# Attention and a routed expert layer on one core: the opening pair in halves, the overflow region moved into a product, the last product cut in columns

## The chip, the cores and the metric

The kernel runs on one core of a Trainium2 chip. A core has a matrix engine (TensorE, PE in the profile; its weight loads are listed apart as PEld), a vector engine (VectorE, DVE), an activation engine (ScalarE, ACT), a general engine (GpSimd, POOL) and a queue engine that mainly starts transfers (SyncE, SP). Each engine works through its own list of instructions in order, and the lists meet only through semaphores. PSUM is the memory that TensorE writes; it is used here in banks of 512 floats per partition.

The metric is the device time of one execution in microseconds. Before the change it is 694.73 us, the median of three runs (694.60 to 694.82).

## The reference

The output is computed in two blocks. Attention comes first, over 4 batches, 8 heads, 768 positions and 64 features. Every query and every key is given to the one of 16 centroids of its head that it resembles most, and a query attends only to keys of its own cluster:

```
q_assign = argmax(q_n @ c_n)          # 16 clusters for each head
k_assign = argmax(k_n @ c_n)
scores   = where(q_assign == k_assign, scale * q @ k.T, -1e9)
attn     = softmax(scores);  x = attn @ v
```

The result, laid out as 3072 rows of 512, goes to a router with 8 experts:

```
expert_idx = argmax((xn @ en.T) / tau);  gate = softmax(...)[expert_idx]
out[row]   = gate * (relu(x[row] @ w1[expert_idx]) @ w2[expert_idx])
```

All inputs are float32. How many rows an expert gets depends on the data.

## The kernel before, in words

**Attention.** The heads are taken two at a time: 4 batches times 4 head pairs are 16 pairs, n = 0 to 15. A pair has 12 units: two halves of the queries (hq, 384 each) by six groups of 128 keys (j). For one unit `scores` (L497) writes a two-bank PSUM tile with two kinds of product. Part 1 is q times k. Part 0 is a bf16 product of code tables (`t["H"]`) that adds a large negative number wherever the clusters differ. `expo` (L526) takes the exponential on ACT into one of six `probs` buffers, and `attend` (L531) multiplies with v on PE and adds the row sums on DVE.

**Preparation of a pair.** Before its scores a pair needs turned q and k, the products with the centroids, the choice of a centroid for every row and the code tables. These are the pieces of `prep_pieces` (L365). For pairs 1 to 15 the pieces are spread over the loop of the pair before (`between`, L1378), q and k are turned by DVE in blocks of 32, and the table is turned by a transposing DMA. Pair 0 has nothing to hide behind: `begin` (L327) does its pieces one after the other, turns q and k with PE (`turn`, L374), multiplies with the centroids (`products`, L403), chooses (`choose`, L422, four DVE instructions on 384 columns), writes codes (`codes`, L435), and turns the table with PE (`turn_numbers`, L459). Then the table's copies, the part 0 products and the first exponentials follow. `keep_up` (L229) issues matmuls whose results nobody reads.

**The order of the work** is written out by hand: under `tc.manual_schedule` every engine's list is the order in which the Python code issues instructions. The main loop after `begin()` takes two units in each step: scores of the two units after next, exponentials, the pieces of `between`, then `attend` of two units. Units 0, 1 and 2 have their scores in `begin`; unit 3 comes in the first step. PSUM is shared out by pools: `psS` has two tiles of two banks (tag `s_ps`), `psO` one, and `misc()` hands out two single banks in turn.

**Experts.** Rows are gathered from the DRAM tensor `x_rows` and results are scattered to `out` by indirect DMAs, which POOL issues. The list `later` has 16 items: "sized" items take one expert each with up to 272 rows, and "block" items take 128 rows of any one expert. Item 13 is a block (positions counted from 0), item 14 the smallest sized item (160 rows) and item 15, the last, is a block. For a block, `hidden` (L1299) computes the 1024 hidden values into two PSUM banks, with one ACT Relu each, and `result` (L1318) multiplies with w2 into one bank `y_ps`, scales on ACT into a tile `y` (three buffers) and scatters. A sized item runs `sized_hidden` (L1210): eight groups (f = 0 to 7) of four products, each group into its own bank, evicted by an ACT Relu (L1227). Three banks come from `psH`, every fourth group goes to `psX`. The weights of an item are in slot 0 or 1 of `w1s` and `w2s`, loaded by SP (2 MB each).

**The overflow region.** If more rows must be placed in blocks than the eight block items can hold, `overflow` (L1589) processes up to 14 more ("whole") items under `tc.If(n_used > KX)`. With these inputs the branch isn't taken. Every engine still loads the count, compares, branches, and then passes a short list of semaphore instructions that stand for the work of the region (these have line L1605, and the loads of the count L1590): first it waits until its own earlier work is done, then it raises its counters to the values that they would have after the region. POOL's list waits for every earlier scatter and gather to land, and ends with an instruction named INC_SWDGE_SEM that raises the counters of the indirect DMAs. Whatever comes after the region and touches a buffer which the region may use waits for the raised counters. In the kernel before, the region is called at L1630, at the head of item 14; the weight loads of item 15 follow it.

Of the kernel before, what the change touches and what calls it, by code (L numbers as in the profile page):

```python
# [18 lines left out]
P = 128  # L19
# [20 lines left out]
def kernel(  # L40
# [143 lines left out]
    def load(n, names):  # L184
        b, hp = pairs[n]
        t = ld.setdefault(n, {})
        for nm in names:
            x = t[nm] = ldp.tile([P, NJ, 2, D], F32, tag=nm + "32", name=nm + "32")
            for h in range(2):
                rows = {"q": q, "k": k, "v": v}[nm][b, 2 * hp + h]  # L190
                if nm == "v":

                    r = rows.rearrange("(i j a t) d -> a i t j d", i=2, a=2, t=SQ)
                    for g in range(P // SQ):
                        nc.sync.dma_start(
                            out=x[SQ * g : SQ * g + SQ, :, h], in_=r[g // 2, g % 2]
                        )
                    continue
                if n == 0:

                    for i in range(1 + (nm == "k")):
                        js = slice(NJ // 2 * i, NJ // 2 * i + NJ // 2) if nm == "k" else slice(0, NJ)
                        queue = nc.scalar if nm == "k" and i == 0 else nc.sync
                        queue.dma_start(
                            out=x[:, js, h], in_=rows.rearrange("(j p) d -> p j d", p=P)[:, js]
                        )
                    continue


# [42 lines left out]
    def constants():  # L252
        nc.vector.memset(onesb, 1.0)
        keep_up(10, idle_ps[:, 0])
# [45 lines left out]
    def unit_centroids():  # L300
        unit_rows(cn_r)
        nc.vector.tensor_scalar(cn2, bc(c_sb, [P, 2, D], 1), cn_r, None, ALU.mult)
        bk = misc()
# [8 lines left out]
    def unit_experts():  # L312
        unit_rows(en_r)
        nc.vector.reciprocal(tau, tau)
        nc.vector.tensor_scalar(emb, emb, en_r, tau, ALU.mult, ALU.mult)

    def turned_experts():
        bk = misc()
        for c in range(KD):
# [3 lines left out]
        nc.vector.tensor_copy(  # L323
            embT[:, :, 0:E], bk[:, 0 : KD * E].rearrange("p (c e) -> p c e", e=E)
        )

    def begin():  # L327

        nc.scalar.dma_start(out=c_sb, in_=centroids.rearrange("h c d -> (h c) d"))
        load(0, "q")  # L330
        load(0, "k")
        nc.sync.dma_start(out=emb, in_=moe_expert_emb)
        nc.sync.dma_start(out=tau, in_=moe_tau.to_broadcast([E, 1]))
# [4 lines left out]
        nc.scalar.activation(en_r, epsc[0:E], ACTF.Sqrt)  # L338
        norm_rows(cn_r, c_sb, P)
        unit_centroids()  # L340
        piece(0, "turn0")
        piece(0, "turn1")
        norm_rows(en_r, emb, E)

        nc.scalar.activation(cn_r, epsc, ACTF.Exp)
        piece(0, "products")
        for m in range(2):
            scores(m, (1,))
        un[2]["s_ps"] = psO.tile([P, 2, 512], F32, tag="o_ps", name="s_ps2")
        scores(2, (1,))  # L350
        piece(0, "choose")
        piece(0, "codes")
        keep_up(6, misc())
        unit_experts()
        rest = piece(0, "turn_numbers")
        next(rest)
        for m in range(3):
            scores(m, (0,))
        next(rest, None)
        turned_experts()  # L360
        for m in (0, 2, 1):
            expo(m)
        token_numbers()

    def prep_pieces(n):  # L365
# [8 lines left out]
        def turn(nm, half):  # L374
# [12 lines left out]
            if nm == "q":  # L387
                (nc.vector.tensor_copy if half else nc.scalar.copy)(
                    t["qT"][:, HS * half : HS * half + HS], bk[:, 0:HS]
                )  # L390
            else:
                (nc.scalar.copy if half else nc.vector.tensor_copy)(
                    in_halves(t["kT"])[:, half], bk[:, 0:HS].rearrange("p (s t) -> p s t", t=SQ)
                )
# [27 lines left out]
        def choose():  # L422
# [3 lines left out]
            amax = smp.tile(shp[0:2], F32, tag="amax", name="amax")  # L426
            sel = smp.tile(shp, BF16, tag="sel", name="sel", bufs=1)
            pm = smp.tile(shp[0:2], BF16, tag="pm", name="pm")
# [6 lines left out]
        def codes():  # L435
            pm = t["pm"]
            nc.scalar.activation(cd[..., 1], pm, ACTF.Copy, scale=wcd)
            for i, p0 in enumerate((0, D)):
                g = slice(p0, p0 + D)
                if n == 0:  # L440
                    nc.vector.scalar_tensor_tensor(
                        out=cd[g, :, :, 2 * i],
# [6 lines left out]
                    continue  # L449
# [4 lines left out]
            if n > 0:  # L454
                nc.sync.dma_start_transpose(
                    out=t["H"], in_=cd.rearrange("p s h c -> p (s h c)")
                )

        def turn_numbers():  # L459

            U = S // (4 * SQ)
            bks = []
            for half in range(2):
                bk = misc().bitcast(BF16)
                for u in range(U):
                    nc.tensor.transpose(
                        bk[:, P * u : P * u + P],
                        cd[:, U * half + u].rearrange("p h c -> p (h c)"),
                        identb,
                    )  # L470
                bks.append(bk[:, 0 : P * U].rearrange("r (s x) -> r s x", x=P))
            H = [t["H"][:, U * half : U * half + U] for half in range(2)]
            nc.vector.tensor_copy(H[0][:, :, 0:SQ], bks[0][:, :, 0:SQ])
            nc.scalar.copy(H[0][:, :, D:], bks[0][:, :, D:])
            nc.vector.tensor_copy(H[1][:, :, 0:SQ], bks[1][:, :, 0:SQ])
            yield
# [822 lines left out]
    def hidden(it, halves=(0, 1)):  # L1299

        d = mo[it]
        for half in halves:
            if half == 0:
                d["hT"] = mop.tile([P, F], F32, tag="hT", name="hT")
# [415 lines left out]
```

## Time and profile before

| quantity | value |
|---|---|
| median of three runs | 694.73 us (694.60 to 694.82) |
| the profiled execution's own time | 695.09 us |
| its span, first to last instruction | 693.3 us |
| granted TensorE clock | 0.999 |
| TensorE busy | 684.1 us, 99% of the span |
| VectorE, ScalarE, GpSimd busy | 381.8, 262.6 and 266.2 us |
| DMA traffic | 135.55 MB, 196 GB/s on average |

The profile is of one execution. Its own time is 1.8 us longer than its span; that is what lies outside the first and last instruction. A line such as "L518 PE MATMUL" is a group of instructions by the line of the kernel that issued them, the engine and the operation. In a timeline a row gives start and length in us, the engine, the line, the operation and its tiles, how many instructions are merged in it and, in brackets, how long the engine was idle before and who ended that. The chain of waits follows the last instruction back from releaser to releaser.

### The profile page before, as it was taken

The numbers are of one execution on the slowest core, as the hardware profiler recorded it, in microseconds if no ns is written. First come the engines' busy times: TensorE is split into PE (matmuls) and PEld (weight loads), VectorE is DVE, ScalarE is ACT, GpSimd is POOL, SyncE is SP. The second block draws the span as 40 slices with busy tenths as digits, with TensorE's granted clock in tenths as the row PEclk, the third lists the DMA queues.
The fourth block names the chain that finished last, engine by engine and source line by source line (L and its number), as shares of the span: only waits on it lengthen the run. The fifth ranks groups of instructions, "written<-read, shape, count | busy, mean of one in ns | idle before, by whom it ended". The sixth has DMA issues, their size and how long they took to land.

```text
span 693.3 us, 16291 instructions
## 1 busy us (share of the span) xinstructions
PE 684.1 (99%) x6517; PEld 459.3 (66%) x6517; DVE 381.8 (55%) x667; ACT 262.6 (38%) x443; POOL 266.2 (38%) x494
## 2 busy tenths in 40 slices
PE   8999999999999999999999999999999999999996
PEld 4444444444444444455866778888979797979694
DVE  5789898999989999988564122140211303030310
ACT  5666665577656765576224120101010111111111
POOL 2122221321232212343315343576656465646502
PEclk9999999999999999999999999999999999999999
DMA  8755556875577588699699957457777686879450
GB/s 133 123 93 105 101 94 95 155 144 103 106 138 157 99 163 162 182 261 271 176 318 359 353 211 269 136 182 283 281 273 279 205 301 228 301 256 315 155 225 32
DMA packets 244157, 135.55 MB, mean 196 GB/s; under 512 B 207840, under 2 KB 207842, under 8 KB 244076
## 3 DMA queue, kind: packets, MB, share of 16 engines
q1 hardware_dynamic: 237116, 121.10, 64.3%
q0 software_dynamic: 6016, 13.12, 5.4%
q8 instruction: 54, 0.88, 0.6%
q10 hardware_dynamic: 944, 0.23, 0.2%
q14 instruction: 27, 0.22, 0.1%
HBM read 115.92 MB, written 13.12 MB: 186 GB/s over the span
## 4 chain that ended last, share of the span: by engine, by line
PE 91%; issue 3%; DMA 3%; POOL 1%; DVE 1%; POOLq 0%; ACT 0%; DVEq 0%
PE s_ps L518 22%; PE o_ps L540 18%; PE h_ps L1309 10%; PE y_ps L1325 10%; PE h_ps L1220 9%; PE y_ps L1258 6%; PE misc L1258 5%; PE x_ps L1220 3%; DMA out_dram<-ys,spidx 3%; PE misc L590 2%; PE misc L411 2%; PE misc L669 1%; PE idle_ps L232 1%; POOL xin L1078 0%; POOL out_dram L1089 0%
## 5 line engine op out<-in xcount | busy, mean ns | idle before, releaser
L529 ACT ACTIVATE prob<-s_ps 128x768 f32<-128x768 f32 x192 | 154.1, 814 | 100.7 <-PE s_ps L518 99.7
L518 PE MATMUL s_ps<-qT,kT 64*64 64x384 f32 x1536 | 155.6, 482 | 0.0
L540 PE MATMUL o_ps<-prob,v 64*64 64x385 f32 x1536 | 141.1, 483 | 0.0
L559 DVE TENSOR_TENSOR acc<-acc,prob 128x768 f32<-128x768 f32 x128 | 121.7, 951 | 8.5
L540 PEld LDWEIGHTS o_ps<-prob,v 64*64 64x64 f32 x1536 | 58.1, 133 | 65.2 <-issue 57.6
L1309 PE MATMUL h_ps<-xTm,w1s 128*128 128x128 f32 x768 | 88.5, 275 | 0.0
L1309 PEld LDWEIGHTS h_ps<-xTm,w1s 128*128 128x128 f32 x768 | 87.5, 192 | 1.4 <-issue 1.0
L1267 DVE STREAM_TRANSPOSE ys<-y_ps 128x256 f32<-128x256 f32 (+4 forms) x16 | 6.2, 404 | 147.0 <-PE y_ps L1258 119.1
L1325 PE MATMUL y_ps<-w2s,hT 128*128 128x512 f32 x192 | 84.5, 593 | 0.0
L518 PEld LDWEIGHTS s_ps<-qT,kT 64*64 64x64 f32 x1536 | 55.2, 133 | 36.9 <-issue 32.3
L574 POOL COPY behind<-acc 1x1 f32<-1x1 f32 x30 | 6.7, 223 | 178.2 <-DVE acc L559 169.3
L1220 PE MATMUL h_ps<-xTs,w1s 128*128 128x272 f32 (+7 forms) x384 | 72.9, 346 | 1.1 <-ACTq L1605 1.1
L1220 PEld LDWEIGHTS h_ps<-xTs,w1s 128*128 128x128 f32 x384 | 66.6, 190 | 8.0 <-issue 2.4
L1316 ACT ACTIVATE hT<-h_ps 128x512 f32<-128x512 f32 x24 | 14.3, 596 | 149.1 <-PE h_ps L1309 121.5
L1089 POOL DMA_INDIRECT out_dram<-ys,spidx x56 | 56.2, 1004 | 35.5 <-DVE ys L1282 18.3
L518 PE MATMUL s_ps<-hot 64*64 64x384 bf16 x768 | 64.2, 325 | 1.0 <-DVE hot L477 0.7
L1078 POOL DMA_INDIRECT xs<-x_rows,gpidx x56 | 56.9, 1016 | 18.7 <-issue 18.1
L1325 PEld LDWEIGHTS y_ps<-w2s,hT 128*128 128x128 f32 x192 | 35.6, 190 | 40.2 <-issue 39.9
L518 PEld LDWEIGHTS <-hot 64*64 64x64 bf16 x768 | 23.8, 106 | 43.9 <-issue 41.8
L1258 PE MATMUL misc<-hTs,w2o 128*128 128x272 f32 (+7 forms) x256 | 48.2, 346 | 0.0
L1258 PE MATMUL y_ps<-hTs,w2o 128*128 128x272 f32 (+7 forms) x256 | 48.0, 346 | 0.0
L1258 PEld LDWEIGHTS misc<-hTs,w2o 128*128 128x128 f32 x256 | 44.4, 190 | 2.7 <-issue 0.2
(274 smaller groups left out, 711.0 us busy)
## 6 DMA issues: line engine op xcount, KB each, us to landing
w1s<-in_moe_w_dram SPq DMA_DIRECT2D x18, 2048.0 KB
w2s<-in_moe_w_dram SPq DMA_DIRECT2D x18, 2048.0 KB
v<-in_v_dram SPq DMA_DIRECT2D x128, 48.0 KB
k<-in_k_dram SPq DMA_DIRECT2D x62, 96.0 KB
q<-in_q_dram SPq DMA_DIRECT2D x60, 96.0 KB
x_rows<-xb SPq DMA_DIRECT2D x60, 96.0 KB
xr<-x_rows SPq DMA_DIRECT2D x9, 512.0 KB
w1s<-in_moe_w_dram SPq DMA_DIRECT2D x4, 1024.0 KB
```

The costliest lines, as they stand in the source:

```text
L411: nc.tensor.matmul(bk[2 * C * i : 2 * C * i + 2 * C, 0:HS], lhsT=cnB[:, hp], rhs=r, start=True, stop=True,)
L518: nc.tensor.matmul(s_ps[D * half : D * half + D, h, 0:HS], lhsT=l[rows, half], rhs=r[rows], start=part == (1 if len(parts) < 2 else 0), st ...
L529: nc.scalar.activation(d["prob"][:, :, 0:HS], d["s_ps"][:, :, 0:HS], ACTF.Exp, scale=scale)
L540: nc.tensor.matmul(g["o_ps"][D * h : D * h + D, half, 0:HE], lhsT=ld[n]["v"][keys, j, h], rhs=d["prob"][keys, h, 0:HE], start=(j == 0), st ...
L559: nc.vector.tensor_tensor(g["acc"], g["acc"], d["prob"][:, :, 0:HS], ALU.add)
L1078: nc.gpsimd.indirect_dma_start(out=to, out_offset=None, in_=of, in_offset=bass.IndirectOffsetOnAxis(ap=at, axis=0), bounds_check=n - 1, oo ...
L1089: inst = nc.gpsimd.indirect_dma_start(out=to, out_offset=bass.IndirectOffsetOnAxis(ap=at, axis=0), in_=of, in_offset=None, bounds_check=n - 1,
L1220: nc.tensor.matmul(bk, lhsT=w1s[it.slot][:, c, P * f : P * f + P], rhs=d["xT"][:, c, 0:C], start=(c == 0), stop=(c == KD - 1),)
L1258: nc.tensor.matmul(bks[g][:, 0:C], lhsT=d["w2"][:, f, P * g : P * g + P], rhs=d["hT"][:, f, 0:C], start=(f == 0), stop=(f == KF - 1),)
L1309: nc.tensor.matmul(bk[:, m : m + P], lhsT=w1s[it.slot][:, c, f0 + m : f0 + m + P], rhs=d["xT"][:, P * c : P * c + P], start=(c == 0), stop ...
L1316: nc.scalar.activation(d["hT"][:, f0 : f0 + 512], bk, ACTF.Relu)
L1325: nc.tensor.matmul(bk, lhsT=d["hT"][:, P * c : P * c + P], rhs=w2s[it.slot][:, c], start=(c == 0), stop=(c == KF - 1),)
```

## The change

Three things change, with some moves that go with them.

1. **The first pair in two halves.** `load` takes pair 0's q and k in halves of 384 rows, all on SP's queue: q first half, k first half, q second half, k second half. v of pair 0 is loaded in the order of its rows, with one DMA for each head instead of four. emb and tau are loaded from ACT's queue. `turn` becomes one piece for each matrix and half and returns its copy, so that `begin` says which engine makes it. kT keeps the rows' order. `half_products`, `choose(half)` and `codes(half)` work on half of the columns; the middle code is computed by POOL instead of ACT for pair 0. The second half's products go to a bank of their own (`c_ps`, in a tile of `psS`). `table(half)` turns six code blocks in two banks of three, with one copy of each bank, where `turn_numbers` had five copies. For pair 0 the part 0 product takes the half's table, so a unit of the first query half needs the first half's table of queries. `begin` interleaves the halves, and only units 0, 2 and 1 are scored there; unit 3's scores now stand between the two `attend` calls of the first step. `keep_up` issues 8 matmuls at the start instead of 10, and the second call, of 6, is gone. The scaling of the experts' embedding goes to one ACT instruction, its copy from PSUM too. `products` of pair 1 move from the first step's end into the second step, and `token_numbers` moves from `begin` to the fifth step.
2. **The region inside a block's second product.** `overflow` is called in item 13 between the two halves of `result`. Inside the region "whole" items use the buffers of others for their hidden values and results (`hTs`, `h_ps`), item 13's slot of weights, and reload half of item 13's w2 at the end. The tile `y` of item 13 is taken in the second half of `result`, and so after the region.
3. **The last product in 384 and 128 columns.** Item 15 uses `result_last`: eight products into one bank for columns 0 to 383, an ACT instruction for these, eight products into the other bank for the last 128 columns, an ACT instruction for those, then the scatter.

The core of the diff:

```diff
+                    for half in halves:
+                        js = slice(NJ // 2 * half, NJ // 2 * half + NJ // 2)
+                        nc.sync.dma_start(out=x_h[:, js], in_=rows[:, js])
...
-        keep_up(10, idle_ps[:, 0])
+        keep_up(8, idle_ps[:, 0])
...
-        piece(0, "turn0")
-        piece(0, "turn1")
-        norm_rows(en_r, emb, E)
-        nc.scalar.activation(cn_r, epsc, ACTF.Exp)
-        piece(0, "products")
-        for m in range(2):
-            scores(m, (1,))
...
-        keep_up(6, misc())
-        unit_experts()
-        rest = piece(0, "turn_numbers")
-        next(rest)
-        for m in range(3):
-            scores(m, (0,))
-        next(rest, None)
-        turned_experts()
-        for m in (0, 2, 1):
-            expo(m)
-        token_numbers()
+        piece(0, "turn", "q", 0)(nc.vector.tensor_copy)
+        piece(0, "turn", "k", 0)(nc.scalar.copy)
+        turned_centroids()
+        unit_experts()
+        nc.scalar.activation(emb, emb, ACTF.Copy, scale=en_r)
+        piece(0, "half_products", 0)
+        piece(0, "turn", "q", 1)(nc.scalar.copy)
+        ld[0]["c_ps"] = psS.tile([P, 2, 512], F32, tag="s_ps", name="c_ps")
+        piece(0, "turn", "k", 1)(nc.scalar.copy)
+        turned_experts()
+        junk = smp.tile([P, 1], F32, name="junk1", bufs=1)
+        nc.scalar.activation(junk, epsc, ACTF.Exp)
+        piece(0, "choose", 0)
+        piece(0, "codes", 0)
+        scores(0, (1,))
+        piece(0, "half_products", 1)
         un[2]["s_ps"] = psO.tile([P, 2, 512], F32, tag="o_ps", name="s_ps2")
         scores(2, (1,))
+        evicts = piece(0, "table", 0)
+        evicts[0](nc.vector.tensor_copy)
+        evicts[1](nc.scalar.copy)
+        scores(0, (0,))
+        expo(0)
+        piece(0, "choose", 1)
+        piece(0, "codes", 1)
+        scores(2, (0,))
+        expo(2)
+        scores(1, (1,))
+        evicts = piece(0, "table", 1)
+        evicts[0](nc.vector.tensor_copy)
+        evicts[1](nc.scalar.copy)
+        scores(1, (0,))
+        expo(1)
...
             for m in range(i, i + 2):
                 attend(m)
+                if m == 0:
+                    scores(3, (1,))
+                    scores(3, (0,))
+                    expo(3)
...
+    def result_last(it):
+        d = mo.pop(it)
+        y = mop.tile([P, DM], F32, tag="y", name="y", bufs=3)
+        cols = [slice(0, DM - P), slice(DM - P, DM)]
+        for cut in cols:
+            bk = bank("y_ps", psY)
+            for c in range(KF):
+                nc.tensor.matmul(bk[:, cut], lhsT=d["hT"][:, P * c : P * c + P],
+                    rhs=w2s[it.slot][:, c, cut], start=(c == 0), stop=(c == KF - 1))
+            nc.scalar.activation(
+                y[:, cut], bk[:, cut], ACTF.Copy, scale=it.gates[:, it.col : it.col + 1])
+        scatter(out[:], it.tables[2][:, it.col : it.col + 1], y, N)
...
+                own.e = expert_of(own)
+                load_part(w2s[own.slot], moe_w2, own.e, KF, 1, 2)
...
             if i == LAST - 1:
-                overflow()
                 weights1(later[LAST])
                 weights2(later[LAST])
...
-                result(it)
+                result(it, (0,))
+                if i == LAST - 2:
+                    overflow()
+                result(it, (1,))
...
-                result(it)
+                result_last(it)
```

## The prediction, made before the change was run

> **What bounds the kernel now.** I read the page first, then the chain of waits over the opening and the timelines of both ends.
>
> The page's first part:
>
> ```profile
> PE 684.1 (99%) x6517; PEld 459.3 (66%) x6517; DVE 381.8 (55%) x667; ACT 262.6 (38%) x443; POOL 266.2 (38%) x494
> ```
>
> TensorE is idle for only 9 us of 693, but part of its busy time in the opening computes nothing. The chain of waits from 0 to 32 us (start, length, what):
>
> ```profile
> 1.07 4.45 PE idle_ps L232 x10
> ...
> 7.85 1.22 PE misc L411 x8
> 9.07 0.02 issue
> 9.09 0.59 DVE asn L420
> ...
> 13.80 0.38 DVE hot L477
> 14.18 0.03 issue
> 14.20 0.39 PE s_ps L518 x4
> 14.59 0.02 issue
> 14.61 0.82 ACT prob L529
> 15.43 0.04 issue
> 15.47 1.00 PE s_ps L518 x12
> ...
> 18.91 1.74 PE s_ps L518 x24
> 20.65 1.29 PE o_ps L540 x16
> ```
>
> From 9.09 to 14.20 the chain runs on DVE: transpose, choice, codes, table copies. From 18.91 on, PE is without a gap, so the start of the second step's `attend` (20.65) is my clock for the opening: what comes earlier there comes off the end. The timeline of the tail:
>
> ```profile
> 654.92 0.69 ACT L1336 ACTIVATE y<-y_ps,slot_gates 128x512 f32<-128x512 f32 x1 [4.12 <-PE y_ps L1325]
> 655.17 0.39 SPq L1128 DMA_DIRECT2D w1s<-in_moe_w_dram  x1
> 655.89 0.97 POOL L1089 DMA_INDIRECT out_dram<-y,sidx  x1 [1.94 <-ACT y L1336]
> 655.99 3.53 PE L1220 MATMUL h_ps<-xTs,w1s 128*128 128x160 f32 x24 [1.10 <-ACTq L1605]
> ...
> 687.69 0.69 ACT L1336 ACTIVATE y<-y_ps,slot_gates 128x512 f32<-128x512 f32 x1 [4.65 <-PE y_ps L1325]
> 688.65 0.97 POOL L1089 DMA_INDIRECT out_dram<-y,sidx  x1 [7.43 <-ACT y L1336]
> ```
>
> At the region PE waits for ACT, which must first do item 13's scaling. The instructions of L1605:
>
> ```profile
> L1605 POOLq EVENT_SEMAPHORE  x5: 17/43/43, 656.7 to 665.4; - x5
> L1605 PEldq EVENT_SEMAPHORE  x1: 51/51/51, 655.1 to 655.1; - x1
> L1605 POOLq INC_SWDGE_SEM  x1: 1230/1230/1230, 665.4 to 665.4; - x1
> ```
>
> POOL stays in the region until 666.7 and nobody minds, since nothing behind it is wanted before 675.
>
> **What the skill says.** "TensorE: Matmul & The Clock Gate", Part 1, gives 426.7 ns between 512-column matmuls while the clock is cold and 215.7 ns warm. The trace agrees: L232's first ten are 427 ns apart, the six at 11.1 us 216 ns; the switch falls at about 5.95 us. "DMA: Bandwidth & Descriptors", section "Issuing engines are not separate DMA queues", says that transfers of all engines run on the same 16 DMA engines and interleave. The trace agrees, harshly: an indirect DMA issued alone has raised its semaphore 2.1 to 2.5 us later, one issued just after a 2 MB weight load after 5.4 to 6.5 us (581.41 to 587.04 behind the load of 579.93; 562.73 to 568.52 behind 561.53). "Runtime: NRT & Kernel Launch", "Instruction fetch mechanics", says a taken branch can stall on a fetch; here ACT's branch at 655.46 is followed by its next instruction at 655.92.
>
> **The opening.** I re-time the new order with measured durations; a half costs about half plus the fixed part (0.55 to 0.30).
> - Eight `keep_up` end at 1.07 + 8 x 0.427 = 4.5. SP's half loads (0.5 us of issue each; 786 KB of q and k had landed by 7.0) land q's first half at about 3.7, k's at 4.9, the second halves at 6.0 and 7.2. Emb and tau precede nothing urgent on ACT; two k loads of 0.5 us leave that queue.
> - Six cold transposes (0.213) and the centroids' end at 6.16. DVE copies q (0.56) and the centroids (0.46) until 6.64. Half products then take 0.55, so DVE's transpose runs 7.2 to 7.55, choice and codes (0.30+0.31+0.21+0.30 and 2 x 0.2, with gaps) to 9.25. Before, the same point was 12.48.
> - ACT meanwhile: expert scaling to 7.6 (0.62), copies of q and k to 8.6 (0.48 each), embT 0.2, exp table load 1.28, ready at 10.3. PE scores units 0 and 2 between, table transposes end about 10.2, DVE's copy 10.4, ACT's 10.8. Unit 0's part 0 follows, its exponential ends at 12.0 (before: 15.43).
> - ACT then runs unit 2 (0.81), a table copy (0.48) and unit 1 to 14.15. PE has `attend` 0, unit 3's scores, `attend` 1 by 14.9, then scores 4 and 5 to 16.5 and pair 1's products (0.85). Those need pair 1's k turned by DVE (0.97), landed at 16.8 before. SP starts that load 2.9 us sooner, since v takes 2 issues instead of 8 (5.25 us); at the rate of before (786 KB in 6.2 us behind v) it lands about 15.5, turned by 16.5. The second `attend` starts about 17.35.
>
> That is 3.3 us before 20.65. A schedule on paper misses handoffs, so I take 0.6 off: **-2.7**. Bounds: -3.3, and -1.2 where pair 1's k lands when it did. Moving `token_numbers` (four DVE instructions, 0.7 us in all) costs nothing as DVE idled 2.8 us before 29.45; without that cover it delays an accumulation that has six buffers of lead. Removing the six `keep_up` frees 1.5 us of PE time that was waiting anyway. A cold clock for one more window would cost about 1 us.
>
> **The region.** (a) PE's last y matmul started at 654.30; the next could have started at 654.73 and started at 655.99: 1.26 us lost. New: the first half's end is 3.44 us earlier and ACT is through (its Relu ended 650.81), so only drain, branch and restart remain: counter raised 0.8 us after the last start (655.10 against 654.30), first load about 0.3 later: 0.76 lost. **-0.5**, between -0.1 and -0.7. The SP list has passed by 647.2.
>
> (b) The new wait. `y` of item 13 is taken after the region, and whole items use all three y buffers. So ACT's scaling waits for raised scatter counters, hence for POOL's region; the program of before shows this wait at item 15's scaling, where POOL is long through. Behind it on ACT stand the eight Relus of item 14, and PE needs the first of them for its fifth group, having four banks. When does POOL pass? Its last scatter before the region goes out at 652.98 and landed at 655.15. But SP's load of w1 for item 15 is held only by PE's passing: it went 0.08 us after PE's counter, so it goes at about 651.73 now, ahead of that scatter instead of behind it. With the delay behind a load, 6.1 us, it lands at 659.1. POOL then took 1.51 us from landing to raised counter (665.16 to 666.68): 660.6. ACT scales (0.69), first Relu (0.30), hops: PE goes on at 661.7. It would get to its fifth group 4.45 us (as from 655.99 to 660.44) after 655.5: 659.95. Stall 1.8 us, **+1.8**; bounds 0 (landing in 2.2 us) and 5 (the 9.3 us that item 13's own scatter took). SP's second load waits for the product's end as before; the scatter of y moves behind the region on POOL, where 10 us of slack cover it.
>
> **The last product.** Its 16 matmul records are 0.429 us apart. Cut: 16 x 0.322 (the spacing of 384 columns in L518) + 16 x 0.112 (128 columns, L1309) = 6.95 against 6.87: +0.08. The second hidden half is wanted 2.6 us after the start, 683.2, and was there at 683.05. The scaling on the path falls from 0.69 to about 0.28 (0.30 for 160 columns, L1227), the first hides behind 1.8 us of products: -0.41. Together **-0.3**, between -0.45 and +0.1.
>
> **The sum.** -2.7 - 0.5 + 1.8 - 0.3 = -1.7. The profiled execution has a span of 693.3 and its own time 695.09; these become 691.6 and 693.4. Its 695.09 is 0.36 above the median 694.73, so the median becomes 693.0.
>
> **The rivals.** The kernel's measurement tells 0.2% (1.39 us) from nothing; 693.34 and 696.12 are the bounds.
> - *No wait at y* (0.22): the scatter slips past the load or ACT gets by. Against it: every scatter of the trace issued after a load waited over 5 us. -3.5: 691.2.
> - *The opening stays bound by transfers* (0.15): pair 1's k or DVE's queue holds the second step, -1.2 instead of -2.7. For it: DMA engines were 0.95 busy from 12 to 24 us; against it, SP's earlier start. 694.5.
> - *Slower* (0.13): the scatter lands as late as the one of 655.89 did, 9.3 us after issue, at 662.3. Then POOL passes at 663.8, PE stalls 5.0: 696.2. It decides from 660.8 on, 7.8 us after issue, where the opening's gain is eaten.
>
> **How the numbers follow.** My forecast (0.50) spans 692.0 to 694.3, two thirds under 693.34. Faster: 0.34 + 0.22 = 0.56. Same: 0.16 + 0.15 + 0.02 = 0.33. Slower 0.11. The range 690.9 to 695.6 leaves out a little of the first rival and most of the last.
>
> **What would show it.** First exponential's end near 12.0 and the second step's `attend` near 18; at item 13 a branch gap of 0.8 us; ACT's y a few us after its product, right after INC_SWDGE_SEM, with a gap on PE between the fourth and fifth group of item 14; a last scaling of 0.28 us. Wrong if y starts with its product, or if DVE's turn of pair 1 ends after 17.

## The result and the profile after

| quantity | before | after |
|---|---|---|
| median, 22 runs of each | 694.60 us | 691.63 us |
| lowest and highest | 694.39, 695.16 | 691.41, 695.12 |
| ratio after to before, 95% interval | | 0.9964 (0.9956 to 0.9972) |
| profiled execution: own time, span | 695.09, 693.3 | 691.77, 690.0 |
| second step's `attend` starts | 20.65 | 18.51 |
| item 13's first product with w2 starts | 647.85 | 645.65 |
| item 14's first product starts | 655.99 | 653.06 |
| last scatter is handed over | 688.65 | 685.38 |

The kernel became 2.97 us faster; the forecast was 1.7 us. Of the 22 executions after, 19 lie between 691.41 and 691.99 and three at 695.00 to 695.12. And the gain doesn't come out the same in every measurement: a later one, told below, gave 693.73 us on a chip where the kernel before takes 694.59. Both have to be explained.

Line numbers from here on are those of the kernel after. `attend` is L576, the scores are L554, the y products L1389 and L1366, the scalings L1400 and L1373, item 14's first product L1256, the region L1677. First the page's line for TensorE and the others:

```profile
PE 681.5 (99%) x6533; PEld 461.2 (67%) x6533; DVE 381.3 (55%) x668; ACT 264.2 (38%) x447; POOL 267.3 (39%) x496
```

There are 16 more matmuls than before, 2.6 us less busy time and a span 3.3 us shorter, so idle time on TensorE shrank by only 0.7 us. Most of the busy time that went did nothing: the two products on zeros that the start lost took 0.85 us, and the six of the second `keep_up` 1.47 us. The chain of waits of the opening (start, length, what) answers to the one shown of before:

```profile
1.06 3.60 PE idle_ps L232 x8
...
9.62 0.81 PE s_ps L554 x8
10.43 0.29 PE misc L502 x3
...
10.81 0.37 DVE hot L508
...
13.23 0.50 PE misc L502 x6
13.72 0.29 PE s_ps L554 x4
14.01 0.65 PE o_ps L576 x8
...
18.51 1.46 PE o_ps L576 x16
```

By the timeline the first product with a table starts at 11.44 (before 14.20), the first exponential at 11.84 (14.61), the first `attend` at 13.84 (16.28). The chain runs over the second half: table of the first half on TensorE, its copy on DVE, then the choice and codes of the second half (11.20 to 13.09), then the second table. The first half's table comes after 0.81 us of scores of unit 2 (the row of 9.62), which stand ahead of it in TensorE's list.

The timeline of the tail (start, length, engine, line, tiles, and in brackets the idle time before and who ended it):

```profile
645.86 0.60 ACT L1356 ACTIVATE hT<-h_ps 128x512 f32<-128x512 f32 x1 [2.98 <-PE h_ps L1349]
648.61 0.97 POOL L1125 DMA_INDIRECT out_dram<-ys,spidx  x1 [0.30 <-issue]
649.38 0.39 SPq L1164 DMA_DIRECT2D w1s<-in_moe_w_dram  x1
649.55 3.67 PE L1389 MATMUL y_ps<-w2s,hT 128*128 128x512 f32 x8 [0.30 <-PEq L1677]
653.06 3.42 PE L1256 MATMUL h_ps<-xTs,w1s 128*128 128x160 f32 x24
653.63 0.69 ACT L1400 ACTIVATE y<-y_ps,slot_gates 128x512 f32<-128x512 f32 x1 [7.18 <-DMA out_dram<-ys,spidx]
...
684.74 0.37 ACT L1373 ACTIVATE y<-y_ps,slot_gates 128x128 f32<-128x128 f32 x1 [1.16 <-PE y_ps L1366]
685.38 0.97 POOL L1125 DMA_INDIRECT out_dram<-y,sidx  x1 [7.20 <-ACT y L1373]
```

The wait that the forecast feared is in the sixth row: ACT's scaling ends 7.18 us of idleness when a scatter lands. But the last scatter went out at 648.61, 0.77 us ahead of SP's load of w1 (649.38), and not behind it. It landed at 651.85. From the region's own instructions:

```profile
L1677 PEldq EVENT_SEMAPHORE  x1: 51/51/51, 649.3 to 649.3; - x1
L1677 POOLq INC_SWDGE_SEM  x1: 1210/1210/1210, 652.2 to 652.2; - x1
```

POOL is through at 653.41, ACT scales at 653.63, and item 14 runs without a gap. With the prediction's 4.45 us from the first product to the fifth group (653.06 to 657.5) and 1.0 us for the scaling and the first Relu, the scaling could have come as late as about 656 (an estimate). Why the scatter was so early shows in the first row: the Relu of the second hidden half (645.86) came 0.31 us after the start of the last matmul that feeds it. In the trace of before the same Relu and the last scatter stand at

```profile
650.21 0.60 ACT L1316 ACTIVATE hT<-h_ps 128x512 f32<-128x512 f32 x1 [5.13 <-remote]
652.97 0.97 POOL L1089 DMA_INDIRECT out_dram<-ys,spidx  x1 [0.30 <-issue]
```

There the Relu started 2.46 us after its last matmul's start (647.74), with TensorE running on and ACT free; the prediction had taken that for granted. From the Relu's start to the last scatter it is 2.75 us in the trace after and 2.76 in the one of before. Below, a Relu is called prompt when it starts 0.31 us after the start of its last matmul, and late when it starts 1.5 us or more after it.

### The profile page after: what moved, and what is told of

Same layout as the page of the kernel before. It is cut to its first block, busy times and chain, and to the rows that moved or that the text cites. A ratio compares the mean times of both kernels' runs of the same rounds, so it can differ in the third digit from the quotient of the medians.

```text
span 690.0 us, 16327 instructions
## 1 busy us (share of the span) xinstructions
PE 681.5 (99%) x6533; PEld 461.2 (67%) x6533; DVE 381.3 (55%) x668; ACT 264.2 (38%) x447; POOL 267.3 (39%) x496
## 4 chain that ended last, share of the span: by engine, by line
PE 90%; issue 5%; POOL 2%; DMA 2%; POOLq 0%; DVE 0%; ACT 0%; DVEq 0%
PE s_ps L554 23%; PE o_ps L576 18%; PE h_ps L1349 10%; PE y_ps L1389 10%; PE h_ps L1256 9%; PE y_ps L1294 5%; PE misc L1294 5%; PE x_ps L1256 3%; PE misc L626 2%; DMA out_dram<-ys,spidx 2%; PE misc L415 1%; PE misc L705 1%; POOL out_dram L1125 1%; PE idle_ps L232 1%; POOL xs L1114 0%
## 5 line engine op out<-in xcount | busy, mean ns | idle before, releaser
L554 PE MATMUL s_ps<-qT,kT 64*64 64x384 f32 x1536 | 156.1, 483 | 0.0
L576 PE MATMUL o_ps<-prob,v 64*64 64x385 f32 x1536 | 141.2, 484 | 0.0
L576 PEld LDWEIGHTS o_ps<-prob,v 64*64 64x64 f32 x1536 | 58.1, 133 | 64.7 <-issue 57.1
L554 PEld LDWEIGHTS s_ps<-qT,kT 64*64 64x64 f32 x1536 | 55.4, 133 | 36.3 <-issue 32.4
L1389 PE MATMUL y_ps<-w2s,hT 128*128 128x512 f32 x176 | 77.7, 594 | 0.3 <-PEq L1677 0.3
L1256 PE MATMUL h_ps<-xTs,w1s 128*128 128x272 f32 (+7 forms) x384 | 72.8, 346 | 0.0
L1256 PEld LDWEIGHTS h_ps<-xTs,w1s 128*128 128x128 f32 x384 | 66.7, 190 | 6.5 <-issue 2.9
L1356 ACT ACTIVATE hT<-h_ps 128x512 f32<-128x512 f32 x24 | 14.3, 595 | 144.3 <-PE h_ps L1349 144.3
L554 PE MATMUL s_ps<-hot 64*64 64x384 bf16 x768 | 64.5, 325 | 0.6 <-ACT hot L508 0.6
L1389 PEld LDWEIGHTS y_ps<-w2s,hT 128*128 128x128 f32 x176 | 32.6, 191 | 37.4 <-issue 37.4
L554 PEld LDWEIGHTS <-hot 64*64 64x64 bf16 x768 | 23.9, 107 | 43.0 <-issue 41.2
```

The lines of the kernel that those rows point to most:

```text
L554: nc.tensor.matmul(s_ps[D * half : D * half + D, h, 0:HS], lhsT=l[rows, half], rhs=r[rows], start=part == (1 if len(parts) < 2 else 0), st ...
L576: nc.tensor.matmul(g["o_ps"][D * h : D * h + D, half, 0:HE], lhsT=ld[n]["v"][keys, j, h], rhs=d["prob"][keys, h, 0:HE], start=(j == 0), st ...
L1256: nc.tensor.matmul(bk, lhsT=w1s[it.slot][:, c, P * f : P * f + P], rhs=d["xT"][:, c, 0:C], start=(c == 0), stop=(c == KD - 1),)
L1356: nc.scalar.activation(d["hT"][:, f0 : f0 + 512], bk, ACTF.Relu)
L1389: nc.tensor.matmul(bk, lhsT=d["hT"][:, P * c : P * c + P], rhs=w2s[it.slot][:, c], start=(c == 0), stop=(c == KF - 1),)
```

## The experiments

Twelve runs on four chips: the first four on one, the next four on a second, three on a third, the last on a fourth. (Which chip the result above was measured on isn't known.) Each is compared with runs of the kernel before on the same chip, whose median there was 694.57 to 694.81 us.

**One part alone.** The opening alone is the kernel after with the other two parts put back:

```
-                result(it, (0,))
-                if i == LAST - 2:
-                    overflow()
-                result(it, (1,))
+                result(it)
...
-                result_last(it)
+                result(it)
```

with `overflow()` again at the head of item 14 and the hidden tile and bank of before.

> The opening alone; region and last product as in the kernel before. Theory A (the gain adds up from three places: opening 2.14, region 0.73, last product 0.24 us in the two profiles): 2.1 us faster than before, ratio 0.9969. Rival B (the opening gives everything, the tail only looks shorter because it runs at another moment): 3.0 us faster, ratio 0.9957.

Measured: 693.07 us (692.67 to 693.84), ratio 0.998 (0.9972 to 0.9987), 1.55 us less than before. In its trace the branch gap at item 14 is back (1.08 us, ended by ACT's branch).

The region alone is the kernel before with the region inside item 13's product (the first four lines above the other way round, and the load of w2 behind the region):

> The kernel before with the region alone moved into item 13's second product. Theory A: 0.7 us faster, the branch gap on PE about 0.5 us instead of 1.26, the Relu of item 13's second hidden half prompt (0.3 us after the last matmul's start instead of 2.4) and the last scatters issued before the w1 load. Rival B: no change. Theory C (that Relu is late for a cause of its own, outside the change): the scatters fall behind the load, POOL passes about 7 us after the branch and PE stalls some 1.8 us between the fourth and fifth group of item 14: 1.3 us slower.

Measured: 695.38 us (694.48 to 698.85), ratio 1.0017 (1.0008 to 1.0025): 0.76 us slower than before, and spread over 4 us, where before spreads over 0.7. In its trace the last scatter goes out at 651.66, 0.47 us behind the load of w1 (651.19). ACT's scaling comes at 659.23, and TensorE stands 0.78 us before the fifth group of item 14. That is the forecast's step (b), to the place.

The last product alone, in the kernel before:

```
-                result(it)
+                result_last(it)
```

> The kernel before with the last product in 384 and 128 columns alone. Theory A: 0.25 us faster, last scaling about 0.37 us long instead of 0.69. Rival B: no change (inside 0.1 us). If the Relu of the last second hidden half stays 1.9 us late, the cut product waits for it at most 0.1 us.

Measured: 694.38 us (694.24 to 694.75), ratio 0.9997 (0.9989 to 1.0006), 0.24 us less by the medians, which the interval can't tell from nothing. The traces agree with it: from the start of the last y product to the last scatter it was 8.03 us before and is 7.79 after.

The three add up to -1.55 + 0.76 - 0.24 = -1.03 us, and the whole change had given -2.97. So either the parts act on each other, or something in them depends on more than the code.

**The buffer that the wait is for.** The kernel after, with item 13's y in a tile of its own:

```
-                y = mop.tile([P, DM], F32, tag="y", name="y", bufs=3)
+                y = (
+                    mop.tile([P, DM], F32, tag="y13", name="y13", bufs=1)
+                    if it is later[-3]
+                    else mop.tile([P, DM], F32, tag="y", name="y", bufs=3)
+                )
```

> The changed kernel, item 13's y in a buffer of its own that the region doesn't use, so that its scaling no longer waits for POOL's region. Theory A (the wait is there, but POOL passes in time since the last scatter goes out before the load): the scaling starts right at its product's end, some 0.4 us sooner, and the time stays within 0.1 us of the changed kernel's 691.6. Rival D (the wait costs PE time in some executions): all executions near 691.5 and none near 695.

Measured: 691.88 us (691.42 to 692.16). In its trace the Relu was late (646.98, 1.78 us after its last matmul's start) and the last scatter came behind the load (649.74 against 649.02), landing at 657.41. But ACT's scaling came at 652.91 with its product and TensorE had no gap. The shared buffer is what makes the late scatter cost anything.

**The scatter held back.** Two fills on GpSimd ahead of item 13's last scatters, in the kernel after:

```
+                if i == LAST - 2:
+                    for _ in range(2):
+                        nc.gpsimd.memset(cd, 0.0)
                 share(i, 1, mo[it]["hT"][0:1, F - 1 : F])
```

> Adds two fills of the dead code tile on GpSimd (about 1.4 us each) ahead of the last scatter work of item 13, so that the last two scatters are handed over after SyncE's 2 MB load of w1 and not before it. Theory of the lost race: they land 5 to 9 us after that load's start, the scaling of item 13's result on ScalarE comes at about 657 to 660 in place of 653.63, TensorE stands still for 1 to 4 us between the fourth and fifth group of item 14's first product, and the time is 693 to 695. Rival, that the wait is covered whenever the load is issued: no gap between these groups, time 691.6 to 692.0.

Measured: 698.04 us (697.55 to 698.86), more than expected. The same fills with the buffer of its own:

> The same two fills, and item 13's result in a buffer of its own, so that nothing that ScalarE does waits for a scatter. If the shared buffer is the whole cost of the late scatters, there is no gap in item 14's first product and the time is 691.4 to 692.0 although the scatters land as late as with the fills alone. If late scatters cost through something else (the region's start on GpSimd, the scatter of item 13's result, the tail), the time stays above 692.5.

Measured: 692.21 us (692.05 to 692.34). The two traces, first with the shared buffer and then with its own:

```profile
661.64 4.93 PE L1256 MATMUL h_ps<-xTs,w1s 128*128 128x160 f32 x24 [3.62 <-ACT hTs L1263]
```

```profile
653.83 0.69 ACT L1404 ACTIVATE y<-y_ps,slot_gates 128x512 f32<-128x512 f32 x1 [5.10 <-PE y_ps L1389]
```

With the shared buffer TensorE stands still for 3.62 us, and then its 24 products take 4.93 us in place of 3.42. With a buffer of its own the scaling follows its product (L1404 there is L1400 elsewhere), although the last scatter goes out even later (652.73 against 652.31). Same fills, same late scatters, 5.8 us apart: the mechanism is settled.

**The table ahead of the scores.** In the kernel after, the first half's table is put ahead of unit 2's scores:

```
-        un[2]["s_ps"] = psO.tile([P, 2, 512], F32, tag="o_ps", name="s_ps2")
-        scores(2, (1,))
         evicts = piece(0, "table", 0)
         evicts[0](nc.vector.tensor_copy)
         evicts[1](nc.scalar.copy)
+        un[2]["s_ps"] = psO.tile([P, 2, 512], F32, tag="o_ps", name="s_ps2")
+        scores(2, (1,))
```

> In the changed kernel's opening, TensorE works on pair 0's third unit of scores from 9.55 to 10.43 us while the four transposes of the first half's table have been ready since 9.74; here the table's transposes and their two copies stand ahead of those scores. Theory that the wait for the table sets the opening (TensorE, then VectorE's copies, then the choice of the second half): the table starts at about 9.8 in place of 10.43, the second step's products with v start 0.4 to 0.6 us earlier than 18.51, and the time falls to about 691.1 from 691.6. Rival, that the loads or the second half's turns set it: the starts stay where they are and the time stays within 0.2 us of 691.6.

Measured: 694.42 us (692.99 to 696.87), where the theories had said 691.1 and 691.6. The opening did what the first of them said; in the chain of waits the copy and the second step's `attend` stand at

```profile
10.32 0.37 DVE hot L508
...
18.03 1.11 PE o_ps L576 x9
```

0.49 and 0.48 us earlier than in the profile after. (TensorE's clock goes from half to full speed at 5.76 us here and at 5.78 in the profile after, so the two can be compared.) The loss is in the tail: Relu at 648.07, the last scatter at 650.84 behind the load (649.34), the scaling at 658.78, and a gap of 2.19 us on TensorE. The code of the tail is that of the kernel after. The windows of that stretch show what made it dearer still (stretch and length, busy time of PE, PEld, DVE, ACT and POOL, the granted TensorE clock, DMA share, GB/s):

```profile
659.00:662.00 3.00, 2.28 (x13) 2.28 (x14) 0.00 (x0) 1.55 (x6) 0.97 (x1) 0.85 1.06 401
662.00:665.00 3.00, 3.00 (x14) 3.00 (x14) 0.00 (x0) 0.35 (x2) 0.00 (x0) 0.58 0.27 105
```

The clock falls to half at 661.12 and comes back at 664.54; 24 products take 5.20 us in place of 3.42. From item 13's first hidden product to item 15's it takes 36.07 us against 31.94 in the profile after, so a gap of 2.19 us cost 4.1. "TensorE: Matmul & The Clock Gate" of the Trainium skill, Part 1, gives the window of the activity monitor as 3413 ns, and the low stretch here is 3.41 us long, but it speaks of a whole idle window, and here a gap of 2.19 us was enough; one of 1.61 us (next run) was not. The fall comes exactly 192 times 3.413 us after the rise at 5.76. In the 3.41 us that end with it TensorE was idle for 2.01 us; in the run with the fills, whose clock also falls at 661.12, for 3.10. In the next run the whole gap of 1.61 us lies within one such window, and no fall follows.

**Ten products on zeros.** `keep_up(10, ...)` in place of 8 in the kernel after:

> The changed kernel with ten products on zeros at the start in place of eight (0.9 us more of TensorE work before the first turns, at the half rate that it has there). If these products are covered by the loads, as the prediction had it, the time stays within 0.3 us of 691.6; if the opening's start lies on TensorE, it rises by up to 0.9. Theory that the few executions of the changed kernel at 695.0 to 695.1 come from a clock that rises one step of 3.41 us later after the shorter warm-up: none of this kernel's executions lies above 694. Rival, that they come from the late scatter: they occur as often as with eight.

Measured: 695.63 us (693.75 to 699.32). The first transposes start at 5.30 in place of 4.45 and the second step's `attend` follows 0.85 us later, so in the new opening `keep_up` lies on the path, and the two products that the change drops are worth 0.85 us. What it was to say of the executions at 695 it can't say: late Relu (649.62), last scatter behind the load, a gap of 1.61 us, and its times are spread over the whole range.

**The kernel after, once more,** unaltered, on a third chip:

> The changed kernel unaltered, once more. Theory that its few executions at 695 are those in which the last two scatters of item 13's shares come behind the load of w1: most executions lie at 691.4 to 692.0, a minority 1 to 7 us higher, and if the profiled one is a high one, its chain shows ScalarE's scaling after 656, a gap on TensorE before the fifth group of item 14's first product and the last two scatters handed over after SyncE's load. Rival, a clock that rises a step later in the opening: the high ones lie together at 695.0 to 695.1, with the opening 3.4 us later and the tail unchanged.

Measured: 691.66 us (691.53 to 692.11), no execution above 692.2. Its Relu at item 13 is prompt (646.19, 0.31 us after the start of the last matmul). Five executions are too few to show a minority of three in 22, so neither theory of the high ones is decided.

On the same chip, the region alone with a buffer of its own, that is the second run's kernel with the edit of the fourth:

> The kernel before with the region alone, as in the run that came to 695.4, but with item 13's result in a buffer of its own. If the shared buffer's wait is what the region costs, what stays is the shorter branch gap, 0.7 to 0.8 us less than before: 693.8 to 694.0, with little spread. If the region costs in another place too, it stays at 694.6 or above.

Measured: 693.61 us (693.43 to 694.05), ratio 0.9986 (0.998 to 0.9993): 0.96 us less than before, with a spread of 0.6. Its Relu was prompt and its last scatter (650.37) ahead of the load (650.99), so this run sizes the shorter branch gap but doesn't test the buffer. From item 13's first hidden product to item 15's it takes 32.01 us against 32.77 before: the region is worth 0.76 us where nothing stalls.

And six products on zeros, `keep_up(6, ...)`, with item 13's y in a buffer of its own:

> The changed kernel with item 13's result in a buffer of its own (691.9) and six products on zeros at the start in place of eight. With ten, the first transposes started 0.85 us later and everything after them with them. If TensorE's own queue still sets the first transposes with eight, six start them up to 0.85 earlier and the time falls to 691.1 to 691.4. If the first loads set them (the first transposes showed no wait with eight, so the loads were there by 4.45), the gain is less, and if the clock rises one step later for the shorter warm-up, the opening grows by about 1 us to 692.5 to 693.

Measured: 693.89 us (691.52 to 696.35), in clusters: six of 14 at 691.5 to 691.8, four at 694.86 to 695.16, four elsewhere. The profiled one is of 696.35. Unit 0's scores there, and the same ones in the profile after:

```profile
9.72 1.56 PE L554 MATMUL s_ps<-qT,kT 64*64 64x384 f32 x8
```

```profile
8.28 0.88 PE L554 MATMUL s_ps<-qT,kT 64*64 64x384 f32 x8
```

Half speed at 9.7 us. The clock rises at 18.83 us in this execution, against 4.78 to 6.99 in the other traces. With six, the products on zeros end before q is there, and the first transposes wait 0.36 us for it. The same section of the skill says that the window runs freely, so that the moment of the rise depends on where in a window the work begins; the onsets of seven traces with the same opening (4.78, 4.78, 5.76, 5.78, 6.10, 6.62, 6.68) agree, though they spread more than the 500 ns either way that it gives. That one busy window is enough, as it also says, isn't so here: TensorE is listed as busy without a break from 6.93 to 14.3, which is more than two windows long and holds one whole window of the execution's own grid (8.59 to 12.00, counted back from 18.83), and it stays slow. What those 7 us lack isn't settled: their products use parts of the array (64x64, 128x32) or small tiles, and some of them are transpositions (7.73 to 9.27).

**The kernel after, a third time,** on a fourth chip:

> The changed kernel unaltered, a third time, on whichever chip. In the traces so far the Relu of item 13's second hidden half came 0.3 us after the last matmul's start in all four that were taken on one chip or in the same session (the changed kernel twice among them), and 1.5 to 2.6 us after it in all nine others, at the same few items. Theory that the chip decides: if the Relus are late here, the last two scatters come behind the load of w1, and the time is 693 to 697 with a spread of 2 us or more; if they are prompt, it is 691.4 to 692.1 with few exceptions. Rival, that the lateness belongs to the program and the changed kernel is always prompt: 691.4 to 692.1 with prompt Relus, on any chip; late Relus with 691.4 to 692.1 would contradict the first theory.

Measured: 693.73 us (693.40 to 697.00; 17 runs of before on that chip: 694.59), ratio 0.9996 (0.9986 to 1.0006). The very kernel that had gained 2.97 us is 0.86 us faster here by the medians, which the interval can't tell from nothing. That is close to the -1.03 to which the three parts had added up, all on a chip with late Relus: the parts do add up, where the Relu is late. Its timeline:

```profile
647.59 0.60 ACT L1356 ACTIVATE hT<-h_ps 128x512 f32<-128x512 f32 x1 [4.37 <-PE h_ps L1349]
649.72 0.39 SPq L1164 DMA_DIRECT2D w1s<-in_moe_w_dram  x1
650.35 0.97 POOL L1125 DMA_INDIRECT out_dram<-ys,spidx  x1 [0.30 <-issue]
656.66 1.25 PE L1256 MATMUL x_ps<-xTs,w1s 128*128 128x160 f32 x8
658.29 0.69 ACT L1400 ACTIVATE y<-y_ps,slot_gates 128x512 f32<-128x512 f32 x1 [10.11 <-DMA out_dram<-ys,spidx]
659.23 3.53 PE L1256 MATMUL h_ps<-xTs,w1s 128*128 128x160 f32 x24 [1.31 <-ACT hTs L1263]
```

The Relu starts 1.70 us after its last matmul's start (645.89), the last scatter goes out 0.63 us behind the load and lands at 656.51, POOL is through at 658.07, and TensorE stands 1.31 us before the fifth group. From item 13's first hidden product to item 15's it takes 33.52 us against 31.94 in the profile after: 1.58 us more.

In all, this Relu was prompt in the profile after and in the three traces of the third chip, and started 1.5 to 2.6 us after its last matmul's start in the ten others. In every trace of a kernel with the moved region, the prompt Relu goes with a last scatter ahead of the load, and the late one with a scatter behind it. The program doesn't decide that: the kernel after had both. Three chips had late Relus throughout and one prompt ones, but each chip was used in one session only, so chip and session can't be told apart. The ten traces with the late Relu also hold fewer records of DMA semaphore updates (7458 to 7620, against 8979 to 9026 in the four others), so more than this signal differs between them, and an influence of the recording isn't excluded.

What delays the signal isn't known. It isn't a general slowness: in the last trace 16 of the 24 Relus of blocks start within 0.4 us of their last matmul's start, the two of the block before item 13 among them (0.31 us). Nor is a late signal confined to some chips: two Relus of earlier blocks start 0.95 and 1.43 us after theirs in all 14 traces.

The version to keep is the fourth run's: 691.88 us (five executions) on a chip whose Relus are late, 0.25 above the kernel after where they are prompt, and 1.85 below it where they are late. With the table put first as well it wasn't run.

## Why the prediction was right and wrong

The direction, and the time within the range of 690.9 to 695.6, were right: 691.63. The middle was 1.4 us too slow, and the forecast's own span (692.0 to 694.3) missed; on the fourth chip 693.73 lies in it. That the result fell into the range is partly luck: the opening gained 0.9 us less than forecast and the wait cost 1.8 us less, and the two errors offset each other in part. Term by term of the sum -2.7 - 0.5 + 1.8 - 0.3:

**The opening, -2.7: about -1.8.** By the start of `hidden` of the last block before item 13, three traces with the old opening beside that of before lie at 607.02 to 607.34 (before: 607.40), and seven with the new one at 604.99 to 605.82; the means are 607.25 and 605.43. The part alone gave -1.55 by the medians. The mechanism was right and the size was off. The working had the second step's `attend` at 17.35, it came at 18.51, and only 0.6 of these 1.16 us were allowed for as handoffs. The step that was mis-sized is the first half's and the second half's choice and codes on VectorE ("a half costs about half plus the fixed part"): from the first transposition to the codes it took 2.41 us (7.33 to 9.74) in place of 2.05 (7.2 to 9.25), since halves of the four instructions take 0.26 to 0.36 us and not 0.21 to 0.31; choice and codes of the second half took 1.89 us (11.20 to 13.09), where the same step of the first had been given 1.70. From there to the table's transposes the working had the time right (0.95, measured 0.98: 9.74 to 10.72), but part of it is a wait that the order makes, not the data: putting unit 2's scores behind the table gave 0.48 us back. The clock isn't what was missed: it rose at 5.78, and the working had it at about 5.95 (for the trace of before, whose own record has 6.13). It moves the opening from one execution to the next, though: with an onset of 4.78 the same opening was 0.4 us earlier. Transfers were no bound: DVE turned pair 1's k at 15.03 to 16.0, ahead of the 16.5 forecast, so the rival of the opening bound by transfers is refuted in the traces.

**The region's gap, -0.5: -0.76.** Right in kind, and a little outside its bounds of -0.1 to -0.7. Restarting took less than reckoned: the counter at 649.3 and the next matmul at 649.55, 0.46 us beyond the matmuls' own spacing in place of 0.76.

**The new wait, +1.8: nothing on the chip of the result, 1.58 on the fourth.** The wait was where the prediction put it. The step that failed is "so it goes at about 651.73 now, ahead of that scatter instead of behind it". The scatter's time, 652.98, was taken as it stood in the trace of before. It hung on a Relu that started 2.46 us after its last matmul in that trace, and that was late in nine of the thirteen others too, but not in the profile after. There the scatter went out at 648.61, 0.77 us ahead of the load, and the first rival ("the scatter slips past the load") came true with 691.2 forecast against 691.63. Where the Relu was late, the numbers of the forecast hold: landing 6.16 us after the scatter's start against 6.1, from landing to the raised counter 1.56 against 1.51, a stall of 1.58 against 1.8. "DMA: Bandwidth & Descriptors", section "Issuing engines are not separate DMA queues", was read rightly here: 3.24 us to land ahead of the load, 6.16 behind it. Only the spread was wider than the working's 5.4 to 6.5 us: the seven traces with the scatter behind the load have 5.6 to 7.7, and scatters of earlier blocks in the trace of before 7.0 to 8.7.

**The last product, -0.3: -0.24.** The run alone can't tell it from nothing; the traces show it. The last scaling takes 0.37 us in place of the 0.28 reckoned.

With the terms as measured, -1.8 - 0.76 + 0 - 0.24 = -2.8, against the -2.97 of the result; with the stall of 1.58, -1.2 against -0.86 on the fourth.

**The slower rival** named a scatter landing after 660.8 as the point from which the gain is eaten. With item 14 some 2.5 us earlier than the working had it, that point is about 658.3. The fills reached it: their scatter landed at 658.93, TensorE stood 3.62 us, and the kernel went to 698.04; singles of the region alone reached 698.85. The rival was underpriced, since it left out that gaps of 2.19 and 3.62 us also cost a stretch at half clock: the 24 products behind them took 1.4 to 1.7 us more than behind the gaps of 1.31 and 1.61 us (3.53).

**The three executions at 695.0 to 695.1** aren't explained. A clock that rises late would do it (the four at 694.86 to 695.16 with six products on zeros can't be due to the wait at y, which that kernel doesn't have), and so would a stall; no trace of them exists.

## What to carry to other kernels

When a moved step takes its place in a race between two queues, compute the margin and ask of each side which wait its time hangs on: here 0.77 us of margin stood on a Relu that starts 0.31 us or 1.5 to 2.6 us after its last matmul, and 2 of the 3 us of gain with it. A buffer of one's own for the result that crosses such a step takes the race out for 2 KB in each partition, whichever way it goes. And when the parts of a change don't add up, repeat the unaltered kernel elsewhere before looking for a cause in the code.

## What the runs showed of the hardware

- A matmul's signal to another engine can come late: the Relu that waits for it started 1.5 to 2.6 us after the matmul's start in place of 0.31, at the same few places of a program, while TensorE went on with later matmuls. That was so on three of the four chips of the experiments; on the other, and in the profile after, only two places earlier in the program had a late one (0.95 and 1.43 us).
- A gap of 2.19 us on TensorE was followed by 3.41 us at half clock, and so was one of 3.62; gaps of 1.31 and 1.61 us were not. The clock fell 1.4 us after the end of the first gap and 0.5 us before the end of the second, in both cases 655.36 us (192 times 3.413) after it had risen.
- An indirect DMA on GpSimd's queue raised its semaphore 3.2 to 3.9 us after its issue where that was up to 0.8 us ahead of a 2 MB load, and 5.6 to 7.7 us after it where it was 0.5 to 2.8 us behind.
- Six 512-column products on zeros and a break of 0.36 us left the clock at half speed until 18.83 us in one execution, through 7 us of small products without a gap; eight and ten without a break raised it between 4.78 and 6.99 us in all traces.
